# A float32 chain of DFT, expert layers and routing on one core: nine instead of eight groups of rows put off into the first routing list

## The chip, the core and the metric

One core of a Trainium2 chip runs the whole program. Its engines work side by side, each on its own queue of instructions in a fixed order: TensorE (PE, with its weight loads as PEld), VectorE (DVE), ScalarE (ACT), GpSimd (POOL) and SyncE (SP, which only issues DMAs). They wait for each other through semaphores. The metric is device microseconds of one execution; lower is better.

## The reference

The input is x of 8 batches x 3072 positions x 256. Three stages follow, all in float32:

```
X = real(fft(fft(x, axis=1), axis=2))               # 24576 rows of 256
x = ((X @ w1) * (X @ w2)) @ w3 @ w_out               # d_ff = 1024
logits = x @ w_gate                                  # 8 experts, 3072 rows each
greedy: highest logits first, each row to one expert, each expert full at 3072
out[rows of e] = relu(x[rows of e] @ w1[e]) @ w2[e]
```

The last two lines need every logit before the first expert can be told its rows.

## The kernel before, in words

Float32 products are made of three matmuls on rounded high and low parts (hi*hi, hi*lo, lo*hi).

**Stage A** (`stage_a`, up to about 1437 us) runs over 48 groups of 512 rows (8 batches x 2 sets x 3 parts) and, in each, over 8 steps f of 128 hidden columns. A step's `front` is 13 matmuls of the transformed rows with CW and SW (lines 220 to 222 and 843), whose results DVE turns into the product `ab`, kept in the tile `qs` (lines 849, 850, 866); ACT and POOL split it into `ah` and `al` (lines 860, 861). Three steps later `back` multiplies these parts by W, which is w3 and w_out and the gate in one (12 matmuls of 264 columns, lines 807, 808, 811), and after eight steps the group's rows (256 columns) and its logits (8 columns) are copied out (lines 918, 919) and stored in the DRAM tensor `xs_d`.

**Groups put off.** For the last `ASIDE` = 8 groups `back` makes only the logits (two matmuls of 512 columns for a step, lines 888 and 889, and one small turn at the group's end, lines 897 to 901). Their `ah` and `al` are kept: those of the last group (`KEPT` = 1) in SBUF, in the places `tabA` and `tabB`, the others are written to the DRAM tensor `away`, 512 KB for a step. The pairs (group, step) are called pieces here: 8 of a kept group and 56 in DRAM, 64 in all.

**Stage B** (`stage_b`) makes the list of rows of each expert (`route`) and the experts' products. While the first list is made there are no expert products to run, so the put-off ones are woven into it by the generator `putoff`: each piece is 12 matmuls of 256 columns (line 1377), handed out four at a time. The list is a chain on DVE: two searches of 8 counts each (DVE line 1089, ACT 1084 and 1085; after each count two tiny matmuls add up over partitions, lines 1104 and 1105, and DVE goes on with their sum, line 1114), then the mask `M`, positions (lines 1231 to 1240), then three parts in each of which DVE builds `oC` and `oR` (lines 1268, 1273, 1276) and PE multiplies them in 64 matmuls (line 1284, `li`). After the third part DVE writes the indices `idx` (1289), and POOL gathers the first 512 rows of the expert out of `xs_d` (line 1413, four indirect DMAs). PE works through its queue in order, so what stands ahead of lines 1104, 1231 or 1284 delays the list.

How many products go between two steps of the list is a sum of the generator's own estimates: each `yield` of `route` adds its microseconds to `spare`, and every four matmuls take `STEP` = 0.26 off it.

A piece from DRAM is loaded by SP into one of four `yo` tiles (even pieces) or one of the four places FA0, FA1, FB0, FB1 (odd pieces), up to `DEEP` = 7 pieces ahead. When a put-off group is complete, ACT copies it to `xo` (line 1358), POOL adds the row numbers (1360), SP stores it to `xs_d` (1361); for rows that occur in a special table SP then overwrites one row from `md` (1364). The gather reads `xs_d` and so waits for the last of these.

The expert's weights are split by `chunk` (ACT 1403, POOL 1405) into places in tabB, FA and FB, which are free only when the pieces there are used up. Two of the eight chunks are made inside the list (`AHEAD` = 2); before the first of them the loop hands out all products that are left.

Of the kernel before, what the change touches and what calls it, by code (L numbers as in the profile page):

```python
# [10 lines left out]
F32R = mybir.dt.float32r  # L11
# [14 lines left out]
NF = FF // 128  # L26
FMAX = 3.4028234663852886e38
XW = 260
ASIDE, KEPT = 8, 1
SHARE = 864  # L30


# [181 lines left out]
def cp(eng, out, in_):  # L214

    return eng.dma_start(f32(out), f32(in_))
# [9 lines left out]
def body(ctx, tc, I, out, nb=NB, dbg=None):  # L226
# [28 lines left out]
    if dbg == "A":  # L255
        nt = 24 * nb
        nc.sync.dma_start(out["L"], L)
        nc.sync.dma_start(out["xs"][:nt * 128], xs_d[:nt * 128])
        return
    stage_b(tc, I, out, k)  # L260


# [758 lines left out]
def stage_b(ctx, tc, I, out, k):  # L1021
# [19 lines left out]
    ex = ctx.enter_context(tc.tile_pool(name="ex", bufs=2))  # L1041
# [286 lines left out]
    def flatten(t):  # L1328
        return t if len(t.shape) == 2 else t.rearrange("p a b -> p (a b)") if len(t.shape) == 3 else t.rearrange("p a b c -> p (a b c)")
# [10 lines left out]
    def putoff():  # L1340

        items = sorted(k.putoff, key=lambda i: (k.putoff[i] is None, i))
        ready, after = [], []
        spots = [flatten(k.own.tile(shape, F32R, name=tag))[:, :1024].rearrange("p (h c) -> p h c", h=2) for tag, shape, _ in T_F]

        def fetch(i):
            n, f = items[i]
            if k.putoff[n, f] is None:
                hl = spots[i // 2 % 4] if i % 2 else ex.tile([128, 2, 512], F32R, name="yo", bufs=PREP + 1)
                cp(nc.sync, hl, k.away[n, f])  # L1350
                k.putoff[n, f] = hl[:, 0], hl[:, 1]
            ready.append(k.putoff[n, f])

        def finish(n, acc):
            j0 = NT - 4 * ASIDE + 4 * n
            for i in range(2):
                xo = ex.tile([128, 2, XW], F32, name="xo")
                act.activation(xo[:, :, :D], acc[i], AF.Copy)
                j = j0 + 2 * i
                pool.tensor_copy(xo[:, :, D:], k.sc["tok"][:, j:j + 2, None].to_broadcast([128, 2, 4]))  # L1360
                nc.sync.dma_start(xrows[j * 128:(j + 2) * 128].rearrange("(i p) d -> p i d", p=128), xo)
            for b, (p, j) in enumerate(DUP):
                if j0 <= j < j0 + 4:
                    nc.sync.dma_start(xrows[j * 128 + p:j * 128 + p + 1, :D], k.md[b:b + 1])

        for i in range(NF + DEEP):
            fetch(i)
        for m, (n, f) in enumerate(items):
            if f == 0:
                acc = [psum.tile([128, 2, D], F32, tag=f"yp{i}", name=f"yp{i}") if m // NF % 2 else  # L1370
                       psum.tile([128, 512], F32, tag="hp", name="hp", bufs=3).rearrange("p (a d) -> p a d", a=2) for i in range(2)]
            if m >= NF and m + DEEP < len(items):
                fetch(m + DEEP)
            hl = ready.pop(0)
            for x, w in ((0, 0), (0, 1), (1, 0)):
                for i in range(4):
                    nc.tensor.matmul(acc[i // 2][:, i % 2], hl[x][:, i * 128:(i + 1) * 128], k.W[w][:, f, :D],
                                     start=f == 0 and x + w == 0 and i % 2 == 0, stop=f == NF - 1 and x == 1, skip_group_check=True)
                if w == 1:
                    for fn in after:  # L1380
                        fn()
                    after = []
                yield
            after = [lambda n=n, acc=acc: finish(n, acc)] if f == NF - 1 else []
        for fn in after:
            fn()

    def weights(wi):
        st = []
        for n in ("e1", "e2"):  # L1390
            t = ex.tile([128, 2 * FF], F32, name="st" + n, bufs=1)
            pool.indirect_dma_start(out=t, out_offset=None, in_=I[n], in_offset=bass.IndirectOffsetOnAxis(ap=wi, axis=0))
            st.append(t)
        return st

    def chunk(st, f):

        res = []
        for i in range(2):
            src = st[0].rearrange("p (k f) -> p k f", k=2)[:, :, f * 128:(f + 1) * 128] if i == 0 else \  # L1400
                st[1][:, f * D:(f + 1) * D].rearrange("p (k f) -> p k f", k=2)
            hl = [ring(f"w{i}{h}", 10, 256, [T_B] + T_F).rearrange("p (k c) -> p k c", k=2) for h in range(2)]
            act.activation(hl[0], src, AF.Copy)
            use("a", 0.31)
            pool.tensor_tensor(hl[1], src, hl[0], op=ALU.subtract)
            res.append(hl)
        return res
# [17 lines left out]
    def due():  # L1425
        todo = [e[1] for e in late if e[0] <= 0]
        late[:] = [[n - 1, fn] for n, fn in late if n > 0]
        for fn in todo:
            fn()
# [78 lines left out]
    FILL = 1.0, 1.0  # L1508
    PREP = 3
    DEEP = 7  # L1510
    STEP = 0.26
    AHEAD = 2
    QUEUE = [2.0] + [0.5] * 7
    HOLD = [-0.5] + [0.0] * 7
    ONP = [9] * 8
    done, which, gens = [], [], []

    def group(ph, g, wait=1):
        xg = gather(done[ph], g, wait)
        oi = ex.tile([128, 4], I32, name="oi", bufs=3)  # L1520
        later(9, lambda: pool.tensor_copy(oi, xg[:, :, D]))
        xh, xl = xparts()
        return {"xg": xg, "oi": oi, "xh": xh, "xl": xl, "last": (ph, g) == (E - 1, G - 1)}
# [32 lines left out]
    with tc.manual_schedule(engines=ALL):  # L1556
        head, wts, st, n = route(0, done), [], None, 0
        more, spare = putoff() if k.putoff else iter(()), 0.0
        while not done:
            v = next(head)  # L1560
            spare += FILL[bool(which)] * max(v, 0.0) + (v == -1) * STEP
            while spare > 0 and more:
                spare -= STEP
                if next(more, 0) == 0:
                    more = None
            if which and st is None:
                st = weights(which[0])
            n += st is not None
            if n > 13 and len(wts) < AHEAD:
                for _ in more or ():  # L1570
                    pass
                more = None
                wts.append(chunk(st, len(wts)))
        for _ in more or ():
            pass
        cur = group(0, 0, 0)
        clock.update(pe=10.0, v=0.0, a=0.0, d=0.0)
        due()
        while len(wts) < NF:
            wts.append(chunk(st, len(wts)))  # L1580
        for kt in range(2):
            turned(cur["xg"], kt, cur["xh"], cur["xl"])
            due()
            due()
        gens.append(x for gen in [head] + [route(ph, done) for ph in range(1, E)] for x in gen)
        for ph in range(E):
            for g in range(G):
                for f in range(NF):
                    if g == G - 1 and f == 0 and ph + 1 < E:
                        while len(done) < ph + 2:  # L1590
                            next(gens[0])
                        st = weights(which[ph + 1])
                    if f == 0 and (ph, g) != (E - 1, G - 1):
                        nxt = group(*((ph, g + 1) if g + 1 < G else (ph + 1, 0)))
                    lists()
                    pend.append((wts, f, first(wts, f, cur["xh"], cur["xl"], f % ONP[ph] == 1), cur))
                    due()
                    lists()
                    if len(pend) > LAG and (ph, g, f) != (E - 1, G - 1, NF - 1):
                        flush()  # L1600
                    if f in (4, 6) and nxt:
                        turned(nxt["xg"], (f - 4) // 2, nxt["xh"], nxt["xl"])
                    due()
                    if g == G - 1 and ph + 1 < E:
                        wnext.append(chunk(st, f))
                cur, nxt = nxt, None
            wts, wnext = wnext, []
        while late:
            due()

        grp = pend[0][3]
        yo = ex.tile([128, 4, D], F32, name="yo", bufs=PREP + 1)
        for i in range(4):
            for w, f, hhl, _ in pend:
                second(w, f, hhl, grp["yp"], [i])
            act.activation(yo[:, i], grp["yp"][i], AF.Copy)
# [30 lines left out]
```

## Time and profile before

| what | value |
|---|---|
| median of 3 runs | 2871.32 us (2869.03 to 2872.54) |
| the profiled execution's own time | 2861.26 us |
| its span, first to last instruction | 2859.5 us |
| PE busy | 2681.1 us, 94% of the span |
| DVE busy | 2194.8 us, 77% |
| POOL busy | 1568.5 us, 55% |
| ACT busy | 1310.1 us, 46% |

The profile is of one execution, some 0.35% shorter than the median of the timed runs. Busy shares are means over stages with different limits: the first list and the end of stage A are a few per cent of the span, and what the change is worth is read there. All times in rows are microseconds from the start of the span.

### The profile page before, as it was taken

What the parts mean: (1) busy time and instruction counts of PE and PEld (TensorE: products, weight loads), DVE (VectorE), ACT (ScalarE), POOL (GpSimd) and SP (SyncE); (2) the same over time, 40 slices, a digit from 0 to 9 for tenths busy, and PEclk for the clock granted to TensorE, in tenths of its full rate; (3) what the DMA queues carried; (4) which work ended last, traced back from release to release, by engine and by line L of the source; (5) the groups of instructions that cost most, each with busy time, mean ns of one, the idle gap of its engine ahead of it and who ended that gap; (6) DMA issues with size and microseconds to landing.
All of it is one profiled execution on the core that took longest, in us unless ns stands there. A gap on an engine that the chain in (4) does not pass through costs nothing.

```text
span 2859.5 us, 52239 instructions
## 1 busy us (share of the span) xinstructions
PE 2681.1 (94%) x19983; PEld 2469.2 (86%) x19983; DVE 2194.8 (77%) x4016; ACT 1310.1 (46%) x2327; POOL 1568.5 (55%) x1536
## 2 busy tenths in 40 slices
PE   4899999999999999999997989999999999989998
PEld 2799999999999999997796878888888888879997
DVE  9787796878878787798877888888888888873222
ACT  3343343444334343444454646556474746533332
POOL 7286675847759494864405336453544445463532
PEclk7999999999999999999998999999999999999999
DMA  5411010101102010135385212131211212111211
GB/s 194 153 46 53 31 53 17 53 31 38 46 24 66 18 53 31 39 114 210 148 281 212 55 53 56 40 84 40 73 49 62 55 61 57 44 60 45 76 46 36
DMA packets 104629, 207.62 MB, mean 73 GB/s; under 512 B 35162, under 2 KB 60426, under 8 KB 99002
## 3 DMA queue, kind: packets, MB, share of 16 engines
q1 hardware_dynamic: 81000, 131.02, 13.7%
q0 software_dynamic: 22144, 72.84, 7.9%
q8 instruction: 158, 2.59, 0.4%
q14 instruction: 93, 0.76, 0.1%
q10 hardware_dynamic: 1234, 0.41, 0.1%
HBM read 118.41 MB, written 80.28 MB: 69 GB/s over the span
## 4 chain that ended last, share of the span: by engine, by line
PE 61%; DVE 29%; issue 4%; ACT 4%; POOL 1%; DMA 1%; DVEq 0%; ACTq 0%; SPq 0%; POOLq 0%
PE yp L1489 11%; PE l L220 6%; PE l L222 6%; PE l L221 6%; DVE oR L1089 4%; PE acc L807 4%; PE acc L811 4%; PE acc L808 4%; PE hp L220 4%; DVE qs L866 3%; PE hp L222 3%; PE hp L221 3%; DVE pm L849 2%; DVE W L1472 2%; PE l L843 2%
## 5 line engine op out<-in xcount | busy, mean ns | idle before, releaser
L861 POOL TENSOR_TENSOR al<-qs,ah 128x512 fp32r<-128x512 f32 x376 | 517.5, 1376 | 422.5 <-ACT ah L860 346.7
L1489 PE MATMUL yp<-FA,W 128*128 128x256 f32 x3040 | 620.0, 285 | 30.0 <-DVE W L1472 20.8
L1489 PEld LDWEIGHTS yp<-FA,W 128*128 128x128 f32 x3040 | 494.5, 189 | 60.5 <-DVE W L1472 24.5
L866 DVE TENSOR_TENSOR qs<-pm 128x512 f32<-128x512 f32 x384 | 400.5, 1043 | 36.3 <-DVE pm L850 1.4
L849 DVE TENSOR_TENSOR pm<-l,qs 128x512 f32<-128x512 f32 x384 | 264.8, 690 | 174.6 <-PE l L222 149.3
L1472 DVE SCALAR_TENSOR_TENSOR W<-hp,W 128x512 fp32r<-128x512 f32 x336 | 231.2, 691 | 207.0 <-ACT W L1468 207.0
L1489 PE MATMUL yp<-FB,W 128*128 128x256 f32 x1520 | 386.8, 281 | 0.0
L847 ACT ACTIVATE qs<-l 128x512 f32<-128x512 f32 x384 | 227.7, 593 | 335.1 <-PE l L222 321.3
L860 ACT ACTIVATE ah<-qs 128x512 fp32r<-128x512 f32 x376 | 236.8, 630 | 301.4 <-DVE qs L866 261.1
L1499 POOL DMA_INDIRECT out_dram<-yo,oi x188 | 200.6, 1067 | 234.4 <-DMA out_dram<-yo,oi 212.7
L220 PE MATMUL hp<-tabA,tabB 128*128 128x512 f32 x768 | 321.9, 419 | 0.0
L1468 ACT ACTIVATE W<-hp 128x512 fp32r<-128x512 f32 x336 | 197.7, 595 | 269.1 <-PE hp L222 249.6
L221 PE MATMUL hp<-tabA,tabB 128*128 128x512 f32 x768 | 303.5, 395 | 7.6 <-DVE tabA L1442 7.6
L807 PE MATMUL acc<-W,ah 128*128 128x264 f32 x1120 | 288.2, 287 | 14.8 <-DVE xo L919 14.8
L1489 PEld LDWEIGHTS yp<-FB,W 128*128 128x128 f32 x1520 | 287.5, 189 | 14.9
L808 PE MATMUL acc<-W,ah 128*128 128x264 f32 x1120 | 286.5, 285 | 0.0
L1089 DVE TENSOR_SCALAR_CACHE_REDUCE oR<-oR,nx 128x1536 uint16<-128x1536 uint16 x196 | 282.0, 1459 | 0.0
L1413 POOL DMA_INDIRECT xt<-xs_d,idx x192 | 209.8, 1093 | 112.4 <-DVE A L1296 51.4
L850 DVE TENSOR_TENSOR pm<-l,qs 128x512 f32<-128x512 f32 x384 | 261.1, 680 | 0.0
L222 PE MATMUL hp<-tabA,tabB 128*128 128x512 f32 x624 | 247.2, 396 | 0.0
L1463 POOL TENSOR_TENSOR W<-xo,W 128x512 fp32r<-128x512 f32 x48 | 71.2, 1483 | 309.9 <-ACT W L1461 309.6
L807 PEld LDWEIGHTS acc<-W,ah 128*128 128x128 f32 x1120 | 211.9, 189 | 17.5 <-DVE xo L919 17.3
(373 smaller groups left out, 7107.8 us busy)
## 6 DMA issues: line engine op xcount, KB each, us to landing
xs_d<-xo SPq DMA_DIRECT2D x96, 260.0 KB
xt<-in_xg_dram SPq DMA_DIRECT2D x24, 1024.0 KB
away<-ah SPq DMA_DIRECT2D x56, 256.0 KB
away<-al SPq DMA_DIRECT2D x56, 256.0 KB
yo<-away SPq DMA_DIRECT2D x28, 512.0 KB
raw<-in_w3t_dram SPq DMA_DIRECT2D x16, 512.0 KB
FA<-away SPq DMA_DIRECT2D x14, 512.0 KB
FB<-away SPq DMA_DIRECT2D x14, 512.0 KB
```

The source lines that it names most:

```text
L220: nc.tensor.matmul(out, ah, bh, start=start, stop=False, skip_group_check=True)
L221: nc.tensor.matmul(out, ah, bl, start=False, stop=False, skip_group_check=True)
L222: nc.tensor.matmul(out, al, bh, start=False, stop=stop, skip_group_check=True)
L807: nc.tensor.matmul(acc[i][:, :264], ah[:, a], W[0][:, f], start=f == 0, stop=False, skip_group_check=True)
L808: nc.tensor.matmul(acc[i][:, :264], ah[:, a], W[1][:, f], start=False, stop=False, skip_group_check=True)
L849: vec.tensor_tensor(pm[:, 0].rearrange("p w c -> p (w c)"), ue, qs, op=ALU.add)
L850: vec.tensor_tensor(pm[:, 1].rearrange("p w c -> p (w c)"), ue, qs, op=ALU.subtract)
L861: (vec if n == k.aside - 1 and f in LAST else pool).tensor_tensor(al, qs, ah, op=ALU.subtract)
L866: return ah, al, parts, lambda: vec.tensor_tensor(ab, pm[:, :, 0], pm[:, :, 1], op=ALU.mult)
L1089: vec.tensor_scalar(jk[:, :n], T[:, :n], nx[:, i:i + 1], None, op0=ALU.is_ge, op1=ALU.add, accum_out=acc[:, i:i + 1])
L1472: vec.scalar_tensor_tensor(hl, hp, 0.0, hh, op0=ALU.max, op1=ALU.subtract)
L1489: nc.tensor.matmul(yp[i], hhl[seq[s][0]][:, t[i]], seq[s][1], start=f == 0 and s == 0 and (i % 2 == 0 or len(yp) == 4), stop=f == NF - 1 a ...
```

## The change

Nine groups are put off instead of eight: the products of one more group (96 matmuls of 264 columns) leave stage A, 16 logit matmuls of 512 columns and a turn of 4 small ones come in their place, its 16 tiles go to DRAM, and 8 more pieces (96 matmuls of 256 columns) come into the first list: 72 pieces. `STEP` goes from 0.26 to 0.31, so that fewer products stand between two steps of the list. The last `TAIL` = 12 pieces use the `yo` tiles alone, which no chunk of weights needs; the loop then hands out only the products ahead of these twelve before it makes the first chunk, and the twelve go on between the parts of the list. They are loaded 3 pieces ahead instead of 7.

```diff
-ASIDE, KEPT = 8, 1
+ASIDE, KEPT = 9, 1
...
         def fetch(i):
             n, f = items[i]
             if k.putoff[n, f] is None:
-                hl = spots[i // 2 % 4] if i % 2 else ex.tile([128, 2, 512], F32R, name="yo", bufs=PREP + 1)
+                hl = spots[i // 2 % 4] if i % 2 and i < len(items) - TAIL else ex.tile([128, 2, 512], F32R, name="yo", bufs=PREP + 1)
...
         for m, (n, f) in enumerate(items):
+            if m == len(items) - TAIL:
+                free.append(True)
...
-            if m >= NF and m + DEEP < len(items):
-                fetch(m + DEEP)
+            ahead = DEEP
+            if len(items) - m <= TAIL + DEEP:
+
+                ahead = max(PREP, min(DEEP, len(items) - TAIL - 1 - m))
+            while m >= NF and got[0] < min(m + ahead + 1, len(items)):
+                fetch(got[0])
...
-    STEP = 0.26
+
+    TAIL = 12
+    STEP = 0.31
...
             if n > 13 and len(wts) < AHEAD:
-                for _ in more or ():
-                    pass
-                more = None
+                while more and not free:
+                    if next(more, 0) == 0:
+                        more = None
                 wts.append(chunk(st, len(wts)))
```

(`free` and `got` are new lists that start empty and as `[0]`; line numbers from 1340 on move by one to nine.)

**PE, between two counts of the search.** Rows of PE from one pair of tiny matmuls (rps) to the next, in the first search. Before:

```order
L1105 MATMUL rps<-cnt_17116,half 128x4
L1377 MATMUL hp<-W_81,yo 128x256 x4
L1377 MATMUL hp<-W_81,FA_17125 128x256 x4
L1377 MATMUL hp<-W_82,FA_17125 128x256 x4
L1377 MATMUL hp<-W_81,FA_17125 128x256 x4
L1377 MATMUL hp<-W_81,yo 128x256 x4
L1377 MATMUL hp<-W_82,yo 128x256 x4
L1377 MATMUL hp<-W_81,yo 128x256 x4
L1377 MATMUL hp<-W_81,FA_17126 128x256 x4
L1104 MATMUL rps<-cnt_17115,blk 128x4
```

The changed kernel, at a like place:

```order
L1105 MATMUL rps<-cnt_17045,half 128x4
L1384 MATMUL hp<-W_82,yo 128x256 x4
L1384 MATMUL hp<-W_81,yo 128x256 x4
L1384 MATMUL hp<-W_81,FA_17055 128x256 x4
L1384 MATMUL hp<-W_82,FA_17055 128x256 x4
L1384 MATMUL hp<-W_81,FA_17055 128x256 x4
L1384 MATMUL hp<-W_81,yo 128x256 x4
L1104 MATMUL rps<-cnt_17044,blk 128x4
```

32 or 28 products between two counts become 24 or 28. Ahead of the first count stand 144 instead of 168, ahead of line 1182 (between the searches) 48 instead of 56, ahead of line 1231 36 instead of 40.

**PE, from line 1240 to the end of the list.** Before, 64 products follow line 1240, and then the 192 matmuls of `li` with no product among them. In the changed kernel 272 products are left after line 1240: 116 ahead of the first part of `li`, 24 inside it, 64 after it, 12 inside the second part and 56 after that. These 56 stand between the last matmul of the second part and the first of the third:

```order
L1284 MATMUL li<-oC,oR 128x48
L1384 MATMUL hp<-W_82,yo 128x256 x4
L1384 MATMUL hp<-W_81,yo 128x256 x8
L1384 MATMUL hp<-W_82,yo 128x256 x4
L1384 MATMUL hp<-W_81,yo 128x256 x8
L1384 MATMUL hp<-W_82,yo 128x256 x4
L1384 MATMUL hp<-W_81,yo 128x256 x8
L1384 MATMUL hp<-W_82,yo 128x256 x4
L1384 MATMUL hp<-W_81,yo 128x256 x8
L1384 MATMUL hp<-W_82,yo 128x256 x4
L1384 MATMUL hp<-W_81,yo 128x256 x4
L1284 LDWEIGHTS oR
```

Before, the last product of all stood ahead of the first part.

**SP, the last loads and stores of the first list.** Before, the last stores of finished groups (xs_d from xo) and the overwritten row (from md) follow the last load:

```order
L216 DMA yo<-away 128x1024
L216 DMA FB_17128<-away 128x1024
L1361 DMA xs_d<-xo 128x2x260 x4
L1364 DMA xs_d<-md 16x16
```

The changed kernel:

```order
L216 DMA FA_17055<-away 128x1024
L1362 DMA xs_d<-xo 128x2x260 x2
L216 DMA yo<-away 128x1024 x8
L1362 DMA xs_d<-xo 128x2x260 x2
L216 DMA yo<-away 128x1024 x4
L1362 DMA xs_d<-xo 128x2x260 x2
L1365 DMA xs_d<-md 16x16
```

The twelve loads of the tail stand behind the stores of the two groups finished before them, and the last store and the `md` row come after the last product.

## Rows read from the trace of the kernel before

**Rows 1.** The page's head.

```profile
span 2859.5 us, 52239 instructions
```

**Rows 2.** PE in order of time, stage A: start, us, what.

```profile
1245.59 0.40 PE L843 MATMUL l<-e,ew 128*128 128x512 f32 x1
...
1248.70 0.39 PE L843 MATMUL l<-e,ew 128*128 128x512 f32 x1
...
1249.51 0.28 PE L222 MATMUL l<-eo,CW 128*128 128x256 f32 x1
...
1419.10 0.39 PE L843 MATMUL l<-e,ew 128*128 128x512 f32 x1
...
1421.22 0.39 PE L843 MATMUL l<-e,ew 128*128 128x512 f32 x1
```

**Rows 3.** DVE in order of time, the same stage; in brackets idle time and its releaser.

```profile
1252.11 0.69 DVE L849 TENSOR_TENSOR pm<-l,qs 128x512 f32<-128x512 f32 x1
...
1256.41 0.76 DVE L919 COPY xo<-acc 128x264 f32<-128x264 f32 x2
...
1260.60 0.69 DVE L849 TENSOR_TENSOR pm<-l,qs 128x512 f32<-128x512 f32 x1
...
1263.23 0.69 DVE L849 TENSOR_TENSOR pm<-l,qs 128x512 f32<-128x512 f32 x1
...
1286.27 0.20 DVE L901 COPY L<-acc 128x32 f32<-128x32 f32 x1
1286.91 0.69 DVE L849 TENSOR_TENSOR pm<-l,qs 128x512 f32<-128x512 f32 x1 [0.44 <-PE l L222]
```

**Rows 4.** Busy time by stretch, us and count: PE, PEld, DVE, ACT, POOL; PE clock, DMA.

```profile
1437.00:1528.00 91.00, 90.47 (x743) 89.43 (x743) 70.90 (x174) 50.41 (x81) 3.29 (x15) 0.98 0.94 337
...
1640.00:1660.00 20.00, 14.70 (x80) 12.64 (x81) 14.91 (x36) 12.98 (x23) 3.24 (x3) 0.91 0.05 14
```

**Rows 5.** The chain that ended last, first list to first expert: start, us, what.

```profile
1436.91 13.38 PE hp L1377 x96
1450.29 8.51 PE yp L1377 x72
...
1528.49 0.68 PE rps L1240 x3
...
1555.79 0.99 POOL xt L1413
...
1574.60 1.28 POOL W L1463
1575.92 0.74 PE yp L1489 x4
```

**Rows 6.** DVE in order of time, the first search.

```profile
1458.95 0.16 DVE L1114 SCALAR_TENSOR_TENSOR j<-rps,xt 128x3 f32<-128x3 f32 x1 [4.90 <-PE rps L1105]
...
1466.94 0.16 DVE L1114 SCALAR_TENSOR_TENSOR j<-rps,xt 128x3 f32<-128x3 f32 x1 [0.53 <-PE rps L1105]
...
1467.48 1.81 DVE L1089 TENSOR_SCALAR_CACHE_REDUCE oR<-oR,nx 128x1536 uint16<-128x1536 uint16 x1
...
1470.87 0.16 DVE L1114 SCALAR_TENSOR_TENSOR j<-rps,xt 128x3 f32<-128x3 f32 x1 [0.40 <-PE rps L1105]
...
1471.40 1.81 DVE L1089 TENSOR_SCALAR_CACHE_REDUCE oR<-oR,nx 128x1536 uint16<-128x1536 uint16 x1
```

**Rows 7.** PE in order of time, after the search, and a later list.

```profile
1528.86 0.77 PE L1377 MATMUL yp<-W,yo 128*128 128x256 f32 x4
...
1542.92 2.74 PE L1284 MATMUL li<-oC,oR 128*128 128x48 bf16 x64 [6.19 <-DVE oC L1276]
...
1711.42 1.76 PE L1284 MATMUL li<-oC,oR 128*128 128x48 bf16 x64 [1.99 <-DVE oC L1276]
```

**Rows 8.** ACT, the copies of a finished group.

```profile
1540.31 1.07 ACT L1358 ACTIVATE xo<-yp 128x512 f32<-128x512 f32 x2
```

**Rows 9.** SP's waits from 1524 to 1560: us in total, times, longest.

```profile
SPq L1364 <- DMA xs_d<-xo: 2.4, 1, 2.4
```

**Rows 10.** POOL's waits on line 1413: ns min/median/max, first and last start.

```profile
L1413 POOLq EVENT_SEMAPHORE  x2: 17/1169/2321, 1543.5 to 1544.2; - x2
```

More of the change, by code (lines that the diff above doesn't have):

```diff
@@ L1342, in putoff @@
         items = sorted(k.putoff, key=lambda i: (k.putoff[i] is None, i))
-        ready, after = [], []
+        ready, after, got = [], [], [0]
         spots = [flatten(k.own.tile(shape, F32R, name=tag))[:, :1024].rearrange("p (h c) -> p h c", h=2) for tag, shape, _ in T_F]
@@ L1352, in fetch @@
             ready.append(k.putoff[n, f])
+            got[0] = i + 1
         def finish(n, acc):
@@ L1515, in stage_b @@
     ONP = [9] * 8
-    done, which, gens = [], [], []
+    done, which, gens, free = [], [], [], []
     def group(ph, g, wait=1):
```

## The prediction

> **What bounds the kernel now.** I read three places, since the change moves work from the end of stage A into the first list. First, stage A where the put-off groups begin: which engine sets a step's pace there. A step with the products by W takes PE 3.11 us, from one L843 to the next; a step with logits alone takes it 2.12 us when nothing holds it [rows 2]. DVE needs about 2.63 us for its part of a step, L849 to L849 [rows 3]. So where products are made PE sets the pace, and where they are put off DVE should. The ninth group from the end sits at the border; its copies stand at 1256.41 [rows 3]. There DVE already runs late: the last matmul that fills `ue` for one step starts at 1249.51 and takes 0.28 [rows 2], and DVE takes that step up only at 1252.11, 2.3 us later [rows 3]. The folding of the next batch falls on DVE in this stretch. Its next wait for PE is the 0.44 us ahead of 1286.91 [rows 3], well inside the stretch of put-off groups.
>
> Second, the first list. The chain of waits goes through the products: 96 take 13.38 us from 1436.91 (part of it while the clock was low), the next 72 take 8.51, which is 0.118 us each [rows 5]. PE is busy 90.47 of 91 us there [rows 4]. DVE waits 4.90 us for the answer to its first count and about half a microsecond for the others [rows 6]. A round of the search that finds PE free takes 1471.40 - 1467.48 = 3.92 us [rows 6].
>
> Third, the list's end and the expert's start. Before, no product is left when the parts of `li` come, and PE idles 6.19 us ahead of the first [rows 7]. The gather starts at 1555.79; from there POOL's own queue runs to L1463 and hands on to PE at 1575.92 [rows 5]. POOL's order behind the gather is unchanged, so whatever delays the gather delays the rest as much.
>
> **The change part by part.**
>
> *Stage A.* PE loses 96 products and gets 16 logit matmuls: 8 steps x (3.11 - 2.12) = 7.9 us less work. That would be the gain if PE set the pace. But in this stretch DVE has no wait for PE to give back, and DVE keeps all its work except the two copies of the group's end (0.76 us) against one small copy of logits (0.20 us) [rows 3]. Gain 0.5 us; bounds 0 and 7.9. I take 0.5, since the rows show DVE late by 2.3 us within the very steps that change. PE cannot run far ahead either: `l` has four buffers, two for a step. The 16 stores of `ah` and `al` (4 MB) go by SP, ahead of nothing that waits.
>
> *The search.* With STEP 0.31, 24 fewer products stand ahead of the first count: 24 x 0.118 = 2.8 us off the 4.90 us wait. The other counts have 24 or 28 products in between, 2.8 to 3.3 us, within the 3.92 us round, so no count waits for products. That takes the wait of 0.53 us towards 0.40 [rows 6], 0.06 us on average over some 14 counts: 0.9 us. Ahead of line 1182 there are 8 fewer products, ahead of line 1231 4 fewer: 0.9 and 0.5 us. In all DVE's chain is 5.1 us earlier, and line 1240 starts at 1528.49 - 5.1 = 1523.4 [rows 5].
>
> *The list's parts.* The price of this is that PE idles 0.6 to 1.0 us in each round, and after line 1240 there are 272 products, not 64. They start 0.37 us behind it (1528.86 against 1528.49 [rows 5, 7]), at 1523.8. 116 of them take 13.7 us, to 1537.5. The first part of `li` is ready at 1542.92 - 5.1 = 1537.8 [rows 7]: so far nothing is lost. Then come 156 products and the first 128 matmuls of `li`. The products take 156 x 0.118 = 18.4 us. The 64 of a part take 2.74 us when the clock is low, as before, and 1.76 us in a later list [rows 7]; PE is now kept busy, so I take 1.76, twice, 3.5 us. The last product ends at 1537.8 + 21.9 = 1559.7. Before, all three parts were done ahead of the gather's 1555.79 [rows 5]; by DVE's pace they would now be done by 1550.7, so PE is the late one from here.
>
> *The last stores.* The gather waits for the last group in `xs_d`. Behind the last product come two ACT copies, 1.07 us [rows 8] and 0.1 until they start; SP's two issues, for which I take 0.1 and 0.4; its wait for that store's landing ahead of the `md` row, 2.4 us [rows 9]; and 2.3 us until POOL, which waits for that row from 1544.2 on, is let go [rows 10]. With 0.2 us to start, 6.6 us. Before, all this lay under the parts of `li`; that cover is gone, since the third part of `li` (1.8 us) and the index end well within it. The gather starts at 1559.7 + 6.6 = 1566.3, 10.5 us later than 1555.79.
>
> *The tail's loads.* SP sends them behind the stores of two finished groups. The first of these waits for ACT, whose copies stand behind the ACT work for the first part of the list; before, copies in that place ended at 1541.4 [rows 8], so 5.1 us earlier, 1536.3. The first tail piece is wanted two pieces into the `li` part, about 1539.5, some 3 us after that. I take no stall; a late load costs 0 to 3 us for the tail as a whole, for the same order at the second group.
>
> *Chunks of weights.* Two are made in the list as before, twelve POOL subtractions stay behind the gather. Nothing changes.
>
> *Sum.* 10.5 - 0.5 = 10.0 us on the profiled execution: 2861.26 to 2871.3 us (span 2859.5 [rows 1] to 2869.5). Against the median of the runs, which is 10.1 us above that execution, 2871.3 + 10.0 = 2881.3 us.
>
> **A rule weighed against it.** In the changed search PE has a short wait in each round, busy about 3.2 of 3.9 us. In the stretch from 1640 to 1660, with PE busy 14.70 of 20 us, the granted clock was 0.91 [rows 4], that is a part of it at 1.2 instead of 2.4 GHz; in the search before it was 0.98 with PE full. The Trainium skill, TensorE: Matmul & The Clock Gate, section on HAM oscillation, says that waits between bursts of matmuls let TensorE fall back to its half clock again and again. By that rule the search would lose time; by rows alone, 0.91 over the 58 us from 1470.87 to 1528.49 [rows 5, 6] is 0.09 x 58 = 5 us of product work lost, of which the idle time of those rounds hides half. That is the fourth case below, not the sum.
>
> **The rivals.**
>
> *PE sets stage A at the border.* Then the full 7.9 us come back and the total is 10.5 - 7.9 = +2.6: 2873.9 us, no change that can be told. For it: PE is busy nearly all the time there too. Against it: DVE's 2.3 us of lateness. It decides if DVE waits for PE anywhere between 1230 and 1286.
>
> *The list's end stays with DVE: faster.* If PE kept up with the parts, the gather would come 5.1 us earlier, with the 0.5: 2865.7 us. This needs the last product by about 1544, so that 6.6 us later DVE's index, 5 us earlier than before, is the last to come. The 272 products and two parts of `li` would have to fit in 20 us, 0.06 us a product, against 0.118 [rows 5]. Only if far fewer products are left after line 1240 than counted can it be.
>
> *The tail is later still.* Loads late by up to 3 us and the clock's 2.5 us add to the sum: +15.5, 2886.8 us. For it: the loads stand in SP's queue behind stores that wait for ACT and POOL, and 3 ahead instead of 7. Against it: each has some 4 us of products ahead of it.
>
> **How the numbers follow.** What a measurement of this kernel can tell from no change is about 0.2%, 5.7 us. Forecast (+10, own range 2876 to 2885) 0.64; later still 0.15; PE sets stage A 0.14; faster 0.07. Slower by over 0.2% is the first two and a little of the third, 0.80; within 0.2% 0.13; faster 0.07. The range leaves out the faster case and the far end of the later one: 2873 to 2887 us; its low end takes in the full gain in stage A.
>
> **What would show it.** Right: DVE's step at the border as long as before; DVE's first wait in the search about 2 us instead of 4.90; PE with waits of 0.6 to 1 us in each round; then no PE wait from line 1240 to the third part of `li`; the gather released by a DMA on `xs_d`, not by DVE's `idx`, some 6.6 us after the last product and about 10 us later than before. Wrong: the first list starting over 3 us earlier than 1436.9, a gather released by `idx`, or waits of PE for `away` loads of more than a microsecond.

## The result and the profile after

| | before | changed |
|---|---|---|
| median of 5 runs | 2871.73 us (2869.03 to 2872.91) | 2887.41 us (2886.07 to 2890.11) |
| ratio | | 1.0052, 95% interval 1.0041 to 1.0063 |
| profiled execution's own time | 2861.26 us | 2890.11 us |
| first list, start to gather | 118.88 us | 135.39 us |

The change makes the kernel slower by 0.52%, 15.7 us; +10.0 us was forecast, with a range that ended at 2887; the median stands 0.4 us past that end. The two profiled executions lie 28.8 us apart, more than the medians do. Of that, 2.7 us came before the ninth group from the end and 8.0 us behind the gather (1303.7 us from there to the end before, 1311.7 us after), where the change touches nothing. The kernel before, profiled once more (e8), took 1303.4 us there, and all kernels of this study took between 1299 and 1316 us. So the parts are compared below from the list's start (the first put-off product, 1436.91 before [rows 5] and 1441.23 after); a time with a + counts from it.

**Stage A, PE in order of time, changed kernel:** the first step of the ninth group from the end, and the first product of the list; start, us, what.

```profile
1223.39 0.40 PE L843 MATMUL l<-e,ew 128*128 128x512 f32 x1
...
1441.23 5.06 PE L1384 MATMUL hp<-W,tabA 128*128 128x256 f32 x22 [0.30 <-DVE L L901]
```

The first of these two in the kernel before:

```profile
1220.65 0.40 PE L843 MATMUL l<-e,ew 128*128 128x512 f32 x1
```

217.84 us lie between them, against 216.26 in the profile of before (to 1436.91): nothing was gained. The eight steps of the ninth group itself became 2.0 us shorter (22.92 instead of 24.94), and the eight after them 4.7 us longer (27.23 instead of 22.49). At the first of those eight PE had filled `ue` at 1247.42 and DVE took it up only at 1253.69, 6.3 us later, where it was 3.2 us late before.

**The search, DVE in order of time, changed kernel.**

```profile
1461.12 0.16 DVE L1114 SCALAR_TENSOR_TENSOR j<-rps,xt 128x3 f32<-128x3 f32 x1 [2.70 <-PE rps L1105]
...
1464.98 0.16 DVE L1114 SCALAR_TENSOR_TENSOR j<-rps,xt 128x3 f32<-128x3 f32 x1 [0.40 <-PE rps L1105]
```

The wait for the first count fell from 4.90 to 2.70 us and that of a round from 0.53 to 0.40 [rows 6].

**Stretches of the search, changed kernel:** busy time and count of PE, PEld, DVE, ACT, POOL; PE clock, DMA share, GB/s.

```profile
1461.00:1488.00 27.00, 24.24 (x193) 22.98 (x192) 23.79 (x62) 20.27 (x32) 0.38 (x2) 1.00 0.95 326
1488.00:1518.00 30.00, 26.97 (x217) 25.96 (x217) 26.05 (x66) 21.84 (x34) 2.21 (x5) 1.00 0.92 324
```

PE now has a tenth of idle time, and the granted clock is still 1.00, 2.4 GHz throughout.

**PE from line 1240 to the end of the list, changed kernel;** in brackets idle time and what ended it.

```profile
1528.43 0.66 PE L1240 MATMUL rps<-xt,T 128*128 128x384 bf16 x3 [0.42 <-ACT T L1233]
...
1540.60 1.68 PE L1384 MATMUL yp<-W,FA 128*128 128x256 f32 x12 [0.66 <-DMA FA<-away]
1543.08 1.67 PE L1384 MATMUL yp<-W,yo 128*128 128x256 f32 x12 [0.80 <-DMA yo<-away]
1544.59 0.57 PE L1284 MATMUL li<-oC,oR 128*128 128x48 bf16 x16
...
1547.57 0.74 PE L1384 MATMUL yp<-W,yo 128*128 128x256 f32 x4 [0.91 <-DMA yo<-away]
...
1556.80 1.70 PE L1384 MATMUL hp<-W,yo 128*128 128x256 f32 x12 [0.43 <-DMA yo<-away]
1559.34 0.74 PE L1384 MATMUL hp<-W,yo 128*128 128x256 f32 x4 [0.84 <-DMA yo<-away]
...
1570.07 1.78 PE L1284 MATMUL li<-oC,oR 128*128 128x48 bf16 x64
```

Line 1240 comes at +87.20, against +91.58 before. Behind it PE waits five times for a load, 3.64 us in all, and the first part of `li` comes 16.16 us after line 1240, not 14.43 as before [rows 5, 7].

**SP in the same stretch, changed kernel:** issues in order of time.

```profile
1532.87 0.32 SPq L216 DMA_DIRECT2D FA<-away  x1
1540.89 0.89 SPq L1362 DMA_DIRECT2D xs_d<-xo  x2
1541.87 13.44 SPq L216 DMA_DIRECT2D yo<-away  x8
```

From 1532.87 to 1541.87 SP issues no load, for 9.0 us. SP's waits from 1524 to 1575 have a row for it, as total, times and longest:

```profile
SPq L1362 <- ACT xo L1359: 13.8, 3, 7.7
```

The DMA engines were not idle in this pause. POOL loads the first expert's weights there (`ste`, 2.1 MB), which stand in queue q0; SP's loads and stores stand in q1. POOL, then the queues from 1530 to 1541 (packets, MB, share), then two stretches with the columns from above:

```profile
1527.54 1.05 POOL L1399 DMA_INDIRECT ste<-in_e_dram,wi  x1 [9.13 <-DVE wi L1224]
1528.89 0.97 POOL L1399 DMA_INDIRECT ste<-in_e_dram,wi  x1 [0.30 <-issue]
```

```profile
q1 hardware_dynamic: 931, 2.25, 57.0%
q0 software_dynamic: 284, 2.08, 46.0%
```

```profile
1530.00:1541.00 11.00, 10.34 (x88) 10.13 (x87) 10.90 (x35) 2.23 (x3) 5.04 (x2) 1.00 1.04 396
...
1548.00:1560.00 12.00, 10.73 (x126) 10.15 (x125) 4.88 (x20) 2.54 (x3) 2.48 (x6) 1.00 0.73 230
```

The engines fall short only later, from 1548 to 1560. The loads that end PE's first two waits were issued ahead of the pause, at 1530.06 and 1531.47, and moved beside the weights; the load behind the third is the first one after the pause.

**The chain that ended last, changed kernel,** from the late loads to the first expert.

```profile
1530.06 10.50 DMA FA<-away
1540.60 1.27 PE yp L1384 x9
1541.87 5.65 DMA yo<-away
...
1553.62 5.68 DMA yo<-away
...
1571.33 2.69 DMA xs_d<-xo
1574.08 1.79 DMA xs_d<-md
1575.90 0.72 issue
1576.62 0.99 POOL xt L1420
...
1597.36 0.74 PE yp L1496 x4
```

The gather is released by the `md` row, no longer by `idx`; it starts at +135.39, 16.5 us later than before. From there to the first expert product it is 20.74 us, against 20.13 before [rows 5].

### The profile page after: what moved, and what is told of

It reads as the page before. It is cut to its first block, busy times and chain, and to the rows that moved or that the text cites. A ratio compares the mean times of both kernels' runs of the same rounds, so it can differ in the third digit from the quotient of the medians.

```text
span 2888.3 us, 52332 instructions
## 1 busy us (share of the span) xinstructions
PE 2693.2 (93%) x20007; PEld 2474.5 (86%) x20007; DVE 2191.2 (76%) x4015; ACT 1309.7 (45%) x2328; POOL 1559.2 (54%) x1534
## 4 chain that ended last, share of the span: by engine, by line
PE 64%; DVE 27%; issue 4%; ACT 2%; DMA 1%; POOL 1%; DVEq 0%; another core or an unknown queue 0%; SPq 0%; ACTq 0%; POOLq 0%
PE yp L1496 13%; PE l L220 6%; PE l L222 6%; PE l L221 6%; DVE oR L1089 4%; PE hp L220 4%; PE hp L222 4%; PE hp L221 4%; PE acc L807 4%; PE acc L811 4%; PE acc L808 4%; DVE qs L866 3%; DVE pm L849 2%; PE l L843 2%; DVE pm L850 2%
## 5 line engine op out<-in xcount | busy, mean ns | idle before, releaser
L807 PE MATMUL acc<-W,ah 128*128 128x264 f32 x1092 | 281.9, 288 | 15.1 <-DVE xo L919 15.1
L808 PE MATMUL acc<-W,ah 128*128 128x264 f32 x1092 | 280.0, 286 | 0.0
```

Of the source, the lines that this page charges most:

```text
L807: nc.tensor.matmul(acc[i][:, :264], ah[:, a], W[0][:, f], start=f == 0, stop=False, skip_group_check=True)
L808: nc.tensor.matmul(acc[i][:, :264], ah[:, a], W[1][:, f], start=False, stop=False, skip_group_check=True)
```

## The experiments

All times of the list are from each kernel's own profile, ratios against runs of the kernel before on the same chip. The expectations call the group at whose first step stage A is measured the tenth from the end; it is the ninth.

| kernel | line 1240 | first `li` | last product | gather | ratio (95% interval) |
|---|---|---|---|---|---|
| before | +91.58 | +106.01 | +99.81 | +118.88 | 1 |
| before again (e8) | +92.74 | +107.17 | +100.97 | +119.49 | one run |
| changed | +87.20 | +103.37 | +129.00 | +135.39 | 1.0052 (1.0041 to 1.0063) |
| e1, STEP 0.26 | +92.25 | +117.71 | +122.21 | +130.06 | 1.0035 (1.0019 to 1.0051) |
| e2, eight groups | +86.11 | +104.93 | +115.96 | +123.34 | 1.0012 (1.0002 to 1.0021) |
| e3, md early | +86.40 | +101.98 | +127.10 | +131.65 | 1.0042 (1.0027 to 1.0058) |
| e4, stores later | +88.80 | +104.53 | +129.09 | +135.58 | 1.0047 (1.0030 to 1.0065) |
| e5, eight, both | +88.44 | +109.54 | +120.59 | +126.62 | 1.0026 (1.0016 to 1.0036) |
| e6, nine, both, 0.26 | +95.34 | +120.69 | +125.19 | +131.84 | 1.0048 (1.0033 to 1.0063) |
| e7, tail alone | +98.26 | +112.74 | +112.90 | +127.59 | 1.0021 (1.0011 to 1.0031) |
| e9, more places | +87.12 | +102.24 | +124.80 | +131.09 | 1.0025 (1.0014 to 1.0036) |
| e10, more places, 0.26 | +92.30 | +109.40 | +113.93 | +122.13 | 0.9993 (0.9983 to 1.0003) |
| e11, eight, more places, md early | +86.16 | +100.62 | +109.89 | +115.96 | 0.9989 (0.9978 to 1.0000) |

**e1, the old spreading.**

```diff
-    STEP = 0.31
+    STEP = 0.26
```

> The changed kernel with STEP back at 0.26, nothing else: as many products between the counts as before, and 160 instead of 272 after line 1240. Theory (the products that are left after line 1240 set the list's end): line 1240 comes 4.4 us later after the list's start than in the changed kernel, at +91.6 us as before, the last product ends at +113 to +116, the gather starts at +119 to +123 instead of +135.4, and the time is 2873 to 2877 us. Rival (the twelve tail pieces cost, by loads that come late behind the stores, however many products are left): PE still waits 3 to 4 us for loads behind line 1240 and the last product comes after +118, 2879 us or more. Rival (the ninth group costs in stage A or in the experts): the list's end comes back as said, but the time stays above 2880.

The list's end came back less than half as far as the theory wanted: the gather at +130.06. Between line 1240 and the first part of `li` stand 140 products, 16.5 us by 0.118; it took 25.5. PE's waits for loads there and behind, 5.73 us, were longer than in the changed kernel. Behind the longest of them the granted clock of TensorE was also down, 0.51 from 1544.80 to 1547.60, that is mostly at 1.2 instead of 2.4 GHz, and the next piece took 2.72 us to the one behind it instead of 1.41:

```profile
1544.85 2.92 PE L1384 MATMUL yp<-W,yo 128*128 128x256 f32 x12 [2.40 <-DMA yo<-away]
```

The first rival named the place rightly: the tail costs by late loads, and here, with the old spreading, it costs more than in the changed kernel.

**e2, eight groups.**

```diff
-ASIDE, KEPT = 9, 1
+ASIDE, KEPT = 8, 1
```

> The changed kernel with eight groups put off again, STEP 0.31 and the twelve tail pieces kept: 176 products after line 1240 instead of 272. Theory: 1240 at +87.2 us after the list's start as in the changed kernel, 96 products of 0.118 us are gone, 11.3 us, so the last product ends at about +111 to +117 and the gather starts at +117 to +121 (changed 135.4, before 118.9); 2869 to 2874 us. Stage A is then 1.6 us shorter at the border than in the changed kernel. Rival (the tail's late loads): the last product after +118, gather after +124, 2877 us or more. Rival (the ninth group gains in stage A, and this is lost here): the list starts later after the eleventh group from the end than in the changed kernel.

Line 1240 at +86.11 shows that the earlier search does not need the ninth group. The gather, though, comes at +123.34, behind the theory's +117 to +121 and just ahead of the rival's +124; PE waits 4.13 us for loads. Against the changed kernel the gather is 12.05 us earlier, where 11.3 was said for the 96 products; the loads differ as well, so this is no price of the products alone.

**e3, the md row in the middle.**

```diff
-key=lambda i: (k.putoff[i] is None, i)
+key=lambda i: (k.putoff[i] is None, 3.5 if i[0] == ASIDE - 2 else i[0], i[1])
```

> The changed kernel with the order of the put-off groups altered: the last group but one of the sequence, which needs the row from md, goes to the fifth place, so that the md row is written in the middle of the search and the last store alone stands behind the last product. Theory (the gather hangs on the last transfer into xs_d): the wait for the store's landing and the md row's own landing go, 2 to 2.5 us; the gather starts 4 instead of 6.4 us behind the last product, 2885 us. Rival (POOL or the index holds the gather just as long): the gather's start does not move, 2887 us.

From the last product to the gather it is 4.55 instead of 6.39 us: the `md` row was worth 1.8 us. The last product came 1.9 us earlier as well, which nobody had said; PE's waits for loads were 2.43 us instead of 3.64.

**e4, stores later in SP's queue.** The two stores of a finished group (and its `md` row) are issued five pieces later.

```diff
-                nc.sync.dma_start(xrows[...], xo)
+                stores.append((xrows[...], xo))
...
+            if f == SLOT and gone:
+                stored(gone.pop(0))
```

> The changed kernel with the stores of a finished group put into SP's queue five pieces later, so that loads no longer stand behind a store that waits for ACT. Theory (the tail's loads are late since SP waits 7.7 us for ACT's copy): PE's waits for loads after line 1240, 3.6 us in all, fall under 1.5, the last product ends 2 to 3 us earlier, 2884 to 2885 us. Rival (the transfers themselves are too slow: four places, 512 KB each, at about 400 GB/s): the waits stay at 3 to 4 us, 2887 us.

The waits for loads fell from 3.64 to 0.75 us, and yet the last product stood at +129.09. The edit brought two costs of its own. Line 1240 came 1.6 us later: PE waited 2.11 us there for ACT's `T`, and ahead of `T` ACT made copies into `xo` tiles that waited for the later stores. ACT in e4:

```profile
1524.71 0.60 ACT L1359 ACTIVATE xo<-yp 128x512 f32<-128x512 f32 x1 [6.82 <-DMA xs_d<-xo]
...
1525.95 0.48 ACT L1233 ACTIVATE T<-rps 128x384 bf16<-128x384 f32 x1
```

And behind PE's wait the granted clock was down, 0.50 from 1528.20 to 1531.00. PE in e4:

```profile
1526.49 0.66 PE L1240 MATMUL rps<-xt,T 128*128 128x384 bf16 x3 [2.11 <-ACT T L1233]
...
1528.22 2.76 PE L1391 MATMUL hp<-W,yo 128*128 128x256 f32 x12
```

The piece at 1528.22 took 2.56 us to the next start, not 1.41. So PE came to the tail's first piece no earlier than in the changed kernel (+106.4 against +106.3), and found it loaded. From line 1240 to the last product it was 40.3 us, 1.5 less than in the changed kernel. SP now waited more for free places, 24.8 us from 1523 to 1572, against 18.8 in the changed kernel from 1524 to 1575.

e4 decides neither for the stores' place nor for the four places: what it took away in waits for loads, it had lost ahead of them.

**e5 and e6, both together,** with eight groups and STEP 0.31, and with nine and 0.26 (edits of e3 and e4).

> Eight groups put off, STEP 0.31 and the tail of twelve pieces as in the changed kernel, stores put into SP's queue five pieces later, and the group with the md row moved to the fifth place. Theory (late loads and the last transfers took what the earlier search gave): line 1240 at +86 to +87 us after the list's start (before 91.6), first li part at +100.5 to +102.5 (104.9 without the later stores), last product at +111 to +113, gather at +115 to +117 against 118.9 before; 0.07 to 0.14% faster than before. Rival (four places and the transfers themselves are too slow): PE waits 2 us or more for loads, gather at +119 or later, no gain.

> Nine groups put off with STEP 0.26, stores put into SP's queue five pieces later, the md row in the middle. Theory (of the 11.2 us that nine groups with STEP 0.26 lost at the gather, most were late loads ahead of the first li part, not the 96 products): first li part at +109.5 to +112 instead of +117.7, gather at +119.5 to +122 instead of 130.1, within 0.1% of before. Rival (96 more products of 0.118 us cost 11 us wherever they stand): gather at +127 or later, 0.3% slower.

Both failed. One wait of PE for a load was 4.60 us in e5 and 4.78 us in e6. The early `md` row, for which SP waits until a store has landed, now stands among the tail's loads in SP's queue; whether this made the long wait was not tried apart. The edits moved the pause and did not end it. Both also hold the later stores of e4, with their cost.

**e7, the tail alone.** Eight groups and STEP 0.26, so that PE's order in the list is that of before.

```diff
-ASIDE, KEPT = 9, 1
+ASIDE, KEPT = 8, 1
...
-    STEP = 0.31
+    STEP = 0.26
```

> Eight groups, STEP 0.26 as before: of the change only the twelve tail pieces in the yo tiles, loaded 3 ahead behind the stores, remain; the order of PE up to the end of the list is that of before. Theory (3 ahead is late only where PE runs products back to back; here most of the tail is handed out among the counts): PE waits under 1 us for loads before line 1240 and up to 3 us behind it, within the 6.2 us that PE idles there before, so the gather starts at +118.5 to +119.5 and the time is that of before. Rival (the store's place in SP's queue holds the loads in the search as well): waits of PE of 3 us or more ahead of line 1240, gather at +122 or later, 0.1% slower.

The rival held, and this was the turn of the study: with not one product moved, the gather is 8 to 9 us later. SP's issues of e7, in order of time:

```profile
1502.91 0.38 SPq L216 DMA_DIRECT2D FA<-away  x1
1511.65 0.88 SPq L1362 DMA_DIRECT2D xs_d<-xo  x2
1512.62 14.17 SPq L216 DMA_DIRECT2D yo<-away  x8
```

PE in e7, a little later:

```profile
1518.29 1.05 PE L1384 MATMUL hp<-W,yo 128*128 128x256 f32 x4 [3.08 <-DMA yo<-away]
...
1530.31 1.20 PE L1384 MATMUL yp<-W,yo 128*128 128x256 f32 x8 [1.02 <-DMA yo<-away]
```

For 9.7 us no load goes out, and here, where the weights are not yet due, the DMA engines do run short, with a share of 0.32 from 1509 to 1512:

```profile
1509.00:1512.00 3.00, 3.00 (x27) 3.00 (x27) 2.50 (x7) 2.97 (x6) 0.00 (x0) 1.00 0.32 131
```

With 3 instead of 7 ahead the next ones are not yet due when the store comes up, so they stand behind it in SP's queue, and the store waits for ACT's copy. The kernel before issues a load every 0.5 to 2 us as a rule in its second search, never more than 3.7 us apart. The list moves 337 GB/s at a DMA share of 0.94 [rows 4]: there is little left to catch up with. Behind the wait of 3.08 us the granted clock was 0.50 as well, from 1518.50 to 1521.90.

**e8, the kernel before again.**

> The kernel before once more, for the spread of its parts from one execution to the next. From the start of the tenth group from the end to the list's start 216 to 218 us, gather at +118.5 to +119.5 us after the list's start, from there to the end 1300 to 1312 us. If the first or the second of these differs by 3 us or more from the first profile, the parts of other runs tell less than assumed.

217.49 us of stage A, the gather at +119.49, 1303.4 us behind it: all as expected.

**e9, e10 and e11, four more places.** The tail's odd pieces go to `tabA`, free once the kept group's first four pieces are used, and loads stay 7 ahead. e10 has STEP 0.26 besides, e11 eight groups and the order of e3.

```diff
+                if i == len(items) - TAIL:
+                    t = flatten(k.own.tile([128, 2, C1N], F32R, name="tabA"))
+                    spots[:] = [t[:, j * 1024:j * 1024 + 1024].rearrange("p (h c) -> p h c", h=2) for j in range(4)]
-                hl = spots[i // 2 % 4] if i % 2 and i < len(items) - TAIL else ex.tile(...)
+                hl = spots[i // 2 % 4] if i % 2 else ex.tile(...)
...
-            if len(items) - m <= TAIL + DEEP:
-                ahead = max(PREP, min(DEEP, len(items) - TAIL - 1 - m))
```

> The changed kernel with four more places for the tail: its odd pieces go to the four places of tabA, which the kept group has left free by then and which no chunk of weights needs; loads stay 7 ahead to the end. Nothing else moves. Theory (the switch from 7 to 3 ahead stops the loads for some 9 us, from +91.6 to +100.6, in a list whose loads run at nearly the rate of the DMA engines, and PE pays for it behind line 1240): PE's waits for loads there fall from 3.6 to under 1 us, the last product ends at +123 to +125.5 instead of 129.0, the gather starts at +129 to +132 instead of 135.4, 0.33 to 0.4% slower than before instead of 0.52%. Rival (the transfers' rate itself is the limit in the list, with or without the pause): the last product at +127 or later, gather at +133 or later.

> The same four places, and STEP back at 0.26: nine groups with the old spreading over the search, without the pause in the loads. Theory (pause): first li part at +108.5 to +111 instead of 117.7, the last product at +114 to +116, gather at +119.5 to +122.5 instead of 130.1; within 0.15% of before. Rival (the 96 products more cost their 11 us whatever the loads do): gather at +128 or later.

> Eight groups put off, STEP 0.31, the same four more places for the tail, and the group with the md row in the fifth place. Theory: line 1240 at +86 to +88 us, first li part at +100.5 to +102.5, the last product at +110 to +113, gather at +114.5 to +117 against 118.9 and 119.5 in the two profiles of before: 0.08 to 0.17% faster than before. Rival (the loads cannot keep up behind line 1240 even so): gather at +118.5 or later, no gain.

All three theories held, with line 1240, gather and ratio in or next to the ranges. The two edits, more places and no narrowing, were not tried apart. PE's only wait for a load behind line 1240 in e9, and SP's issues there:

```profile
1542.84 1.68 PE L1384 MATMUL yp<-W,yo 128*128 128x256 f32 x12 [0.67 <-DMA yo<-away]
```

```profile
1535.13 3.16 SPq L216 DMA_DIRECT2D yo<-away  x2
1541.74 0.88 SPq L1365 DMA_DIRECT2D xs_d<-xo  x2
1542.71 0.49 SPq L216 DMA_DIRECT2D yo<-away  x1
```

The store still waits for ACT until 1541.7, but loads go out ahead of it until 1538.0, and the pause is 4.7 instead of 9.0 us. The DMA engines fall less short behind it than in the changed kernel's like stretch, where they had 0.73 and 230 GB/s:

```profile
1548.89:1560.89 12.00, 12.00 (x162) 11.83 (x159) 6.21 (x20) 2.55 (x3) 2.86 (x7) 1.00 0.87 326
```

The gather moved by 4.3 us for this alone (+135.39 to +131.09), and by 7.9 us at STEP 0.26 (+130.06 in e1 to +122.13). e10's ratio cannot be told from 1. e11 takes the gather to +115.96 and is the only kernel of the study whose interval lies wholly at or under 1, by 0.11%. Its list is again set by DVE at the end, PE in order of time:

```profile
1524.29 0.66 PE L1240 MATMUL rps<-xt,T 128*128 128x384 bf16 x3 [0.42 <-ACT T L1233]
...
1551.55 1.76 PE L1284 MATMUL li<-oC,oR 128*128 128x48 bf16 x64 [1.91 <-DVE oC L1276]
```

The times of e9 and e10 are 4 to 5 us better than their gathers say; behind the gather executions on that chip took 1309 to 1316 us, and single profiles do not explain such differences.

**e12, DVE's work doubled at the border.**

```diff
+        for _ in range(2 if n in (0, 1) else 1):
             vec.tensor_tensor(pm[:, 1]..., ue, qs, op=ALU.subtract)
```

> The changed kernel with the subtraction of line 850 done twice in the 16 steps of the first two put-off groups, 0.60 us each, 9.6 us more work for DVE there and none for the others. Theory (DVE sets the pace where the ninth group was put off, which is why 7.9 us less work of PE gave nothing): from the start of the tenth group from the end to the list's start 223 to 227.5 us instead of 216.7 to 218.6. Rival (DVE has slack there, and something else took the gain): 220 us or less. The list itself is not touched.

The two subtractions of one step, DVE of e12, and the two ends of the stretch, PE of e12:

```profile
1234.22 1.41 DVE L851 TENSOR_TENSOR pm<-l,qs 128x512 f32<-128x512 f32 x2
```

```profile
1217.52 0.40 PE L843 MATMUL l<-e,ew 128*128 128x512 f32 x1
...
1440.88 5.36 PE L1385 MATMUL hp<-W,tabA 128*128 128x256 f32 x32 [0.30 <-DVE L L902]
```

The second one costs 0.73 us (one takes 0.68), 11.7 us in 16 steps and not the 9.6 that were expected. The stretch took 223.36 us, 5.5 more than in the changed kernel, so a little under half of it reached the end; where PE's 7.9 us were taken away, nothing did. DVE sets much of the pace there; what sets the rest is not shown.

## Why the prediction was right, and where a size was off

**Stage A: right.** Forecast -0.5 us. The first step of the ninth group from the end to the list's start took 216.3 to 217.6 us in six profiles with eight groups (mean 217.3) and 216.7 to 218.6 us in seven with nine (mean 217.8; e12 is not among them). No gain, if not a loss of half a microsecond. The rival that had PE set the pace needed -7.9; e12 and DVE's lateness of up to 6.3 us show why it failed.

**The search: right.** Line 1240 was to come 5.1 us earlier; it came 4.4 us earlier against one profile of before, 5.5 against the other.

**The list's parts: right in kind.** 272 products behind line 1240 were to make PE the late one and move the last product far behind DVE's work. They did. The forecast had 36.3 us from line 1240 to the last product (1559.7 - 1523.4); with eight places, in e9, it was 37.7. The experiments also part the 16.5 us of the gather, by single profiles that agree within 0.6 us for the kernel before: nine groups with the old STEP and the loads put right (e10) cost 3.2 us, STEP 0.31 on top of that 9.0 (e9), the late loads 4.3 (the changed kernel). With nine groups, then, the spreading cost more than the ninth group did: what the search gained, about 5 us, was lost again and more in the products that it left behind line 1240. With eight groups, STEP 0.31 and the loads put right, e11 (which also has the `md` row early) shows no such loss.

**The tail's loads: the term that was mis-sized.** "I take no stall; a late load costs 0 to 3 us for the tail as a whole." In the changed kernel it was 41.8 us from line 1240 to the last product, and 4.1 of the 5.5 us too many vanish in e9. The sign that was named for it, no wait of PE from line 1240 to the third part of `li`, did not come: there are five. The waits shown are 3.64 us; by the starts of the pieces (1.41 us apart where there is no wait) they cost about 4.7 us.

The store's wait itself was foreseen: ACT's copies were said to end at 1536.3, +99.4, 3 us ahead of need, and they ended at 1541.33, +100.1. What the 3 us left out is the load's own time. The first load behind the store was issued at +100.6 and reached the PE that waited for it 5.65 us later, and the three pieces ahead of it give only 3 x 12 x 0.118 = 4.2 us. A second thing had no term at all: the expert's weights, which move through the same DMA engines just then, and beside which a load issued ahead of the pause took 10.50 us. How much of the 4.1 us is due to the places, how much to the narrowing and the store, was not tried apart. The row with a DMA share of 0.94 was there [rows 4], and it was read for its clock alone.

**The last stores: right.** 6.6 us was said from the last product to the gather, 6.39 was measured; e3 shows that 1.8 of it is the `md` row.

**The clock: no part of it in the changed kernel.** The fourth case took 2.5 us from a falling clock in the search. The granted clock was 1.00 in both stretches of the search and on to the end of the list, with PE idle a tenth of the search. The Trainium skill, TensorE: Matmul & The Clock Gate, section on HAM oscillation, tells of waits for loads between bursts of matmuls that bring the clock down again and again; the waits of its kernel are several times as long as those of the search here, so it was not the rule for this case, and the trace does not speak against it. That case's 2886.8 us is near the measured time, and its loads were late, but its half from the clock did not come: that the number fits is in part luck.

**The sum.** The forecast of the list was +10.5 us from its start to the gather (10.0 with stage A's gain of 0.5 counted in); +16.5 was measured. Of the 6.0 us too many, 5.5 stand between line 1240 and the last product, most of them the loads, and 0.7 in a search that came 4.4 instead of 5.1 us earlier; the last stores took 0.2 less. Carried to the timed runs: +15.7 (from the median of 2871.32 that the forecast started from, the ratio gives 2886.3 us). That is outside the forecast's own 2876 to 2885 and nearest to the rival "the tail is later still", which was given 0.15.

## What to carry to other kernels

Where a stretch streams operands from DRAM at nearly the rate of the DMA engines, compare a load's own time, from issue to use, with the work that stands ahead of its use, and count what else moves through the DMA engines just then: a change of the places or of the depth of prefetch can cost time even if no product moves. A prefetch that narrows at its end should narrow into places that were free in time, as `tabA` was. And work put off out of a stage is a gain only if the engine that loses it sets the pace there; a doubt is settled by giving the other engine more work.

## What was not expected of the hardware

Loads of 512 KB for which PE waited had been issued 5.65, 5.68 and 10.50 us before, the last of them while 2.1 MB of weights moved beside it. And a late load costs more than the wait that the profile shows on PE. In the changed kernel each of the five waits put its piece off by more than the wait shown, the first by 0.82 us where 0.66 are shown. In e1, e4 and e7 the granted clock stood at half behind waits of 2.40, 2.11 and 3.08 us, and the products behind them took about twice as long; in the changed kernel, whose longest wait there was 0.91 us, it stayed at 1.00.
